# A new list order for a gated long convolution and MLP kernel, made with SyncE's issues and all transfers each in one line of measured times

## The chip, the cores and the metric

One core of one Trainium2 chip. The metric is the device time of one execution in microseconds (us), the median of the runs. PE is TensorE (PEld its weight loads), DVE is VectorE, ACT is ScalarE, POOL is GpSimd and SP is SyncE, which issues most of the DMAs.

## The reference

Everything is bf16, with S = 2048 rows of D = 512 channels. The normalized input goes through a gated long convolution (A) and is then gated by a GeGLU MLP (B) of the raw input:

```python
x  = A_q
xn = _layernorm(x)
s  = _A_ref(xn, A_k, A_v, A_shift_k, A_ssm_k, A_ssm_D)
g  = _silu(_B_ref(xn, B_w_gate, B_w_up, B_w_down))
return x + s * g

# _A_ref(q, k, v, shift_k, ssm_k, ssm_D)
kv  = (4-tap causal convolution of k along S with shift_k) * v
y_f = rfft(kv, length 2*S) * rfft(ssm_k, length 2*S)      # per channel
y   = irfft(y_f)[:S] + kv * ssm_D
return q * y

# _B_ref(x, w_gate, w_up, w_down): 512 -> 1792 -> 512
return (gelu(x @ w_gate) * (x @ w_up)) @ w_down
```

## The kernel before, in words

The 2048 rows are 16 tiles of 128 rows (t), in 4 quarters (q) of 512 rows. The kernel does two things at once and meets at the end.

*The MLP.* For each quarter, DVE takes the statistics of a tile (L811, L812), POOL the inverse root (L821, L822), and DVE writes the normalized tile XN (L825). The tile is turned to xnT: quarters 0 and 1 on PE (L844) with an eviction from PSUM, quarters 2 and 3 by a transposing DMA (L836). A unit (q, m), m = 0 to 13, is a gate stage of 4 matmuls and an up stage of 4 (through L609, a helper), a gelu on ACT into GE (L1093) and a product on DVE into HT (L1096). The down stages of a quarter follow, in three pieces per tile; ACT takes the gate's tanh (L1120) or silu (L1128), and DVE finishes it (L1122, L1130, L1131).

*The convolution* is a discrete Fourier transform of length 4096 by matmuls in two stages. The first stage multiplies with the table F1; its results go to staging in SBUF, from there to DRAM (ZH for ssm_k, ZK for kv), and come back with the axes changed (BH, BK). ssm_k is first turned on PE (Hn to HTr, L868). Groups H0 to H7 (ssm_k) use four staging slots that lie in the memory of XN and X tiles 8 to 15, so the profile shows them under these names; groups K0 to K7 (kv) use three slots (AST). The second stage works on 32x32 tiles (`tiles`, L984): stages psf0 to psf7 on ssm_k and psk0 to psk7 on kv, evicted to HS and KB. A DMA swaps the halves of HS into HW, DVE multiplies, and the inverse stages psi0 to psi7 (also L984) go through BO, ZI in DRAM and BI to the last transform psy0 to psy7, whose result DVE multiplies into G and, with the MLP's gate, into the output. The inverse table MI is made by turning TF on ACT (`m_turn`, L719) and two transposing DMAs (L995); G1 is a transposed copy of F1.

*PSUM* has 8 banks. Gate, up, down and half stages take one bank, stages of the convolution two neighbouring ones, transposes one. Evictions go through `copy` (L600 on ACT, L603 on DVE).

*What sets the order.* `S.add` collects 780 tasks, each with the engines that may run it and a planned duration. `SEQ`, a list of task numbers, gives the order in which they are emitted; a suffix b takes the second engine of a task. Each engine runs its tasks in this order, and the semaphores between engines are added by `Trk`. `Sched.run` walks the list and keeps planned times. These have one effect on the program: a task that needs a slot of a pool (PSUM banks, staging, GE, HS and others) gets the one that the plan has free first. Loads of inputs ("loads") and most other DMAs are issued by SP, the stores to ZH and ZI by ACT; `dma` (L581) is the helper of both.

In the plan of before, loads have a counter of their own, other transfers share a second one, `pipe`:

```python
elif t.nbytes:
    en = t.end
    if en < self.SHARED:
        free["loads"] += self.TAKEN
    pipe = max(pipe, en + self.DMA_LAT / 2) + t.nbytes / (self.SHARE_BW if en < self.SHARED else self.DMA_BW)
    t.end = pipe + self.DMA_LAT / 2 + (self.WAIT if en < self.SHARED else 0.0)
```

Task numbers that matter below: 130 and 131 are the copy of H6's second half and its store; 116 the copy of H4's second half; 119 and 121 the copies of H5's first quarters; 82 is `m_turn`; 226 and 221 are copies of the second halves of K1 and K0; 233 is the first stage of K3 on PE.

Of the kernel before, what the change touches and what calls it, by code (L numbers as in the profile page):

```python
# [24 lines left out]
N_WARM = 11  # L25
ORDER = "x00 h0 h1 x01 w0 w1 h2 h3 D0 w2 s0 k0 v0 x1 w3 k1 v1 d0 d1 k2 v2 k3 v3 x2 x3"
SEQ = (
# [22 lines left out]
)  # L50
NF_BANKS = 4
ISSUE = 470.0
LOAD_NS = {("x0_", 262144): 800.0, 262144: 850.0, 524288: 1350.0, ("x", 524288): 2100.0, ("h", 524288): 1400.0, ("wg", 524288): 1550.0, ("wu", 524288): 1450.0, 917504: 2620.0, ("sk", 524288): 1500.0, 344064: 1250.0, 46080: 350.0, 3072: 100.0, 1024: 200.0}
W_XT, W_SW, W_BK, W_BH, W_ZI, W_BI, W_ZK, W_MI, W_G1 = 1665000, 600000, 555000, 703000, 333000, 640000, 490000, 740000, 222000
NC_PAIRS = 4
SMALL = 1.15 * 262144
# [235 lines left out]
class Sched:  # L292
# [4 lines left out]
    LOAD_LAT = 2450.0  # L297
    HEDGE = 600.0
    DMA_BW = 370.0
    SHARE_BW = 300.0  # L300
    FIRST = {"loads": 300.0, "SP": 30500.0}
    DRAIN = 121.0
    EARLY, TAKEN, SHARED, WAIT = (2500.0, 1.6), 1400.0, 46000.0, 3300.0
    LANDS = (3850.0, 5450.0, 7050.0, 8650.0, 9600.0, 10450.0)

    def __init__(self):
        self.tasks = []
# [35 lines left out]
                t.deps.append(d)  # L343

    def run(self):
        free = dict(self.FIRST)
        pipe = 0.0
        n_loads = 0
        order = []
        pmode = 0  # L350
        for name in SEQ.split():
            t = self.tasks[int(name.rstrip("b"))]
            eng, dur = t.opts[name[-1] == "b"]
            base = 0.0
            for d in t.deps:
                base = max(base, d.end if eng == d.eng == "PE" else d.end + d.lat + (self.SEM if not d.nbytes or eng != "PE" else 400.0 if d.eng == "loads" else self.HEDGE))
            for b in t.w:
                if b.pool is not None and b.slot is None:
                    f, b.slot = b.pool.find()
                    b.pool.take(b.slot)  # L360
                    base = max(base, f + self.SEM)
            t.start, t.eng = max(base, free.get(eng, 800.0)), eng
            free[eng] = t.end = t.start + dur + (self.DRAIN if eng == "PE" and t.mode != pmode else 0.0)
            pmode = t.mode if eng == "PE" else pmode
            if eng == "loads":
                free[eng] = t.start + dur * (self.EARLY[1] if t.start < self.EARLY[0] else 1.0)
                if n_loads < len(self.LANDS):
                    free[eng] = self.LANDS[n_loads] - self.LOAD_LAT
                n_loads += 1
                t.end = free[eng] + self.LOAD_LAT  # L370
            elif t.nbytes:
                en = t.end
                if en < self.SHARED:
                    free["loads"] += self.TAKEN
                pipe = max(pipe, en + self.DMA_LAT / 2) + t.nbytes / (self.SHARE_BW if en < self.SHARED else self.DMA_BW)
                t.end = pipe + self.DMA_LAT / 2 + (self.WAIT if en < self.SHARED else 0.0)
            for b in set(t.r + t.w):
                b.left -= 1
                b.last_end = max(b.last_end, t.end + t.lat)
# [19 lines left out]
def build_kernel(nc, A_q, A_k, A_v, A_shift_k, A_ssm_k, A_ssm_D, B_w_gate, B_w_up, B_w_down, out):  # L399
    with ExitStack() as es0:  # L400
# [184 lines left out]
        def load(name, out_ap, in_ap, w_res, w_buf, nbytes, ring="SP", r=(), rb=()):  # L585
            sem = dsem("d_" + name)
            ns = LOAD_NS.get((name.rstrip("0123456789"), nbytes)) or LOAD_NS[nbytes]
            last_load[0] = S.add([("loads", ns)], lambda e: dma(ring, out_ap, in_ap, sem, r, w_res), r=rb, w=w_buf, nbytes=nbytes)
# [654 lines left out]
```

## Time and profile before

| | before |
|---|---|
| median of 3 runs | 195.75 us (195.61 to 195.95) |
| span of the profiled execution | 193.77 us |
| time around the span (median less span) | 1.98 us |
| PE busy | 189.6 us, 98% of the span |
| DVE busy | 160.6 us, 83% |
| ACT busy | 120.7 us, 62% |
| data moved by DMA | 48.14 MB, mean 248 GB/s |
| granted PE clock | 1.0 (9 of 9 tenths in all 40 slices) |

The profiled execution has no device time of its own on record; the median of the runs stands in for it beside its span. The span runs from the first to the last instruction. "Busy" is the time in which an engine executes instructions; PEld runs beside PE. The views used are the page, the table by windows, the chain of work that ended last, the groups of instructions by shape, the DMA issues and the timeline.

### The profile page before, as it was taken

What the parts mean: (1) busy time and instruction counts of PE and PEld (TensorE: products, weight loads), DVE (VectorE), ACT (ScalarE), POOL (GpSimd) and SP (SyncE); (2) the same over time, 40 slices, a digit from 0 to 9 for tenths busy, and PEclk for the clock granted to TensorE, in tenths of its full rate; (3) what the DMA queues carried; (4) which work ended last, traced back from release to release, by engine and by line L of the source; (5) the groups of instructions that cost most, each with busy time, mean ns of one, the idle gap of its engine ahead of it and who ended that gap; (6) DMA issues with size and microseconds to landing.
All of it is one profiled execution on the core that took longest, in us unless ns stands there. A gap on an engine that the chain in (4) does not pass through costs nothing.

```text
span 193.8 us, 3522 instructions
## 1 busy us (share of the span) xinstructions
PE 189.6 (98%) x1393; PEld 87.0 (45%) x1393; DVE 160.6 (83%) x246; ACT 120.7 (62%) x168; POOL 12.6 (7%) x32
## 2 busy tenths in 40 slices
PE   7999999999999999999999999999999999999993
PEld 2777444444444444443334334343344444444442
DVE  6998899899989797987996697887796871579984
ACT  5789877598794797874578666668656622150031
POOL 5322400000000000020200000000000000000000
PEclk9999999999999999999999999999999999999999
DMA  6999999999575659999999927788244305938643
GB/s 177 335 376 300 357 376 392 405 386 368 239 222 164 211 142 288 386 296 278 305 326 208 318 88 230 260 276 271 110 166 162 108 3 171 369 88 278 231 166 108
DMA packets 34502, 48.14 MB, mean 248 GB/s; under 512 B 8499, under 2 KB 27191, under 8 KB 34486
## 3 DMA queue, kind: packets, MB, share of 16 engines
q1 hardware_dynamic: 28982, 39.53, 63.1%
q10 hardware_dynamic: 5504, 8.39, 11.8%
q8 instruction: 11, 0.18, 0.4%
q14 instruction: 5, 0.04, 0.1%
HBM read 27.39 MB, written 14.68 MB: 217 GB/s over the span
## 4 chain that ended last, share of the span: by engine, by line
PE 94%; DVE 2%; DMA 2%; POOL 0%; ACT 0%; issue 0%
PE psall L609 86%; PE psall L984 5%; DMA X<-in_A_q_dram 2%; PE psall L868 1%; PE psall L844 1%; DVE XN L825 0%; DVE stats L811 0%; DVE HTr L603 0%; POOL mv L822 0%; DVE G L1131 0%; DVE G L1130 0%; ACT G L1128 0%; DVE xnT L603 0%; POOL mv L821 0%; DVE mv L812 0%
## 5 line engine op out<-in xcount | busy, mean ns | idle before, releaser
L609 PE MATMUL psall<-xnT,Wu 128*128 128x512 bf16 (+1 forms) x232 | 55.8, 372 | 0.0
L609 PE MATMUL psall<-xnT,Wg 128*128 128x512 bf16 (+1 forms) x232 | 55.5, 372 | 0.0
L609 PE MATMUL psall<-Wd,HT 128*128 128x512 bf16 (+2 forms) x238 | 52.7, 367 | 0.0
L1096 DVE TENSOR_TENSOR HT<-psall,GE 128x512 bf16<-128x512 f32 x54 | 36.2, 684 | 11.9 <-PE psall L609 10.9
L1093 ACT ACTIVATE GE<-psall 128x512 bf16<-128x512 f32 x54 | 31.2, 601 | 11.3 <-PE psall L609 9.0
L609 PEld LDWEIGHTS psall<-Wd,HT 128*128 128x128 bf16 x238 | 22.1, 98 | 26.2 <-issue 1.9
L609 PEld LDWEIGHTS psall<-xnT,Wg 128*128 128x128 bf16 x232 | 22.1, 98 | 25.8 <-issue 1.8
L609 PEld LDWEIGHTS psall<-xnT,Wu 128*128 128x128 bf16 x232 | 21.9, 98 | 25.7 <-issue 2.1
L600 ACT ACTIVATE HS<-psall 128x1024 bf16<-128x1024 f32 x15 | 14.7, 1022 | 5.2 <-PE psall L984 5.2
L600 ACT ACTIVATE BO<-psall 128x1024 bf16<-128x1024 f32 x10 | 10.0, 1023 | 10.6 <-PE psall L984 10.5
L600 ACT ACTIVATE KB<-psall 128x1024 bf16<-128x1024 f32 x10 | 10.0, 1023 | 7.7 <-PE psall L984 7.7
L965 DVE TENSOR_TENSOR KTM<-KK,SKB 128x2048 bf16<-128x2048 bf16 x12 | 14.6, 1214 | 0.1
L967 DVE TENSOR_TENSOR KAC<-KAC,KTM 128x2048 bf16<-128x2048 bf16 x12 | 14.6, 1213 | 0.0
L600 ACT ACTIVATE AST<-psall 128x1024 bf16<-128x1024 f32 x12 | 12.1, 1021 | 2.4 <-PE psall L609 2.1
L1120 ACT ACTIVATE G<-psall 128x512 bf16<-128x512 f32 x12 | 7.0, 599 | 10.4 <-PE psall L609 9.9
L1122 DVE SCALAR_TENSOR_TENSOR G<-G,psall 128x512 bf16<-128x512 bf16 x12 | 7.9, 683 | 6.3 <-ACT G L1120 6.3
L1047 DVE TENSOR_TENSOR HS<-KB,HS 128x1024 bf16<-128x1024 bf16 x16 | 10.8, 683 | 1.1 <-ACT KB L600 1.0
L603 DVE CAST BO<-psall 128x1024 bf16<-128x1024 f32 x6 | 7.3, 1225 | 5.3 <-PE psall L984 5.2
L1128 ACT ACTIVATE G<-psall 128x512 bf16<-128x512 f32 (+2 forms) x5 | 2.5, 511 | 14.1 <-PE psall L609 14.1
L811 DVE BATCH_NORM_STATS2 stats<-X 128x6 f32<-128x512 bf16 x16 | 10.4, 675 | 0.7 <-DMA X<-in_A_q_dram 0.7
L1047 DVE TENSOR_TENSOR HW<-KB,HW 128x1024 bf16<-128x1024 bf16 x16 | 10.8, 682 | 0.0
L600 ACT ACTIVATE XN<-psall 128x1024 bf16<-128x1024 f32 (+1 forms) x10 | 8.4, 856 | 2.9 <-PE psall L609 2.8
(81 smaller groups left out, 179.4 us busy)
## 6 DMA issues: line engine op xcount, KB each, us to landing
BH<-ZH SPq DMA_DIRECT2D x8, 512.0 KB, 5.8
HW<-HS SPq DMA_DIRECT2D x16, 256.0 KB, 3.0
BK<-ZK SPq DMA_DIRECT2D x8, 512.0 KB, 5.9
ZI<-BO ACTq DMA_DIRECT2D x16, 256.0 KB, 2.5
BI<-ZI SPq DMA_DIRECT2D x8, 512.0 KB, 4.5
ZK<-AST SPq DMA_DIRECT2D x6, 512.0 KB, 3.0
Hn<-in_A_ssm_k_dram SPq DMA_DIRECT2D x4, 512.0 KB, 6.4
KK<-in_A_k_dram SPq DMA_DIRECT2D x4, 512.0 KB, 10.8
```

What stands on the lines that cost most here:

```text
L600: return h.activation(o, i, ACTF.Copy, scale=scale)
L603: return h.tensor_copy(o, i)
L609: return h.matmul(o, lhsT=l, rhs=r, start=st, stop=sp)
L811: t_stats[t] = op([("DVE", 670.0)], lambda e, h, t=t: h.bn_stats(stats[:, t, :], X[:, t, :]), r=[bX[q][t % 4]], w=[bst[t]], rr=[R_X[t]], w ...
L965: op([("DVE", dur)], lambda e, h, j=j, m=m: h.tensor_tensor(KTM[:, m.slot, :, :], kk(j), sk(j), ALU.mult), r=need + [bSKB[j], a], w=[m], r ...
L967: op([("DVE", dur)], lambda e, h, m=m: h.tensor_tensor(KAC[:, a.slot, :, :], KAC[:, a.slot, :, :], KTM[:, m.slot, :, :], ALU.add), r=[m], ...
L984: trk.op("PE", lambda h: h.matmul(ps(s, i)[b, :], lhsT=wt(col)[a, :], rhs=data(col)[a, :], start=n < 16, stop=n >= len(todo) - 16, tile_po ...
L1047: return hd.tensor_tensor(o, flat(KB, kb[h]), o, ALU.mult)
L1093: op([("ACT", act(512))], lambda e, h: h.activation(GE[:, g.slot, :], bank(pg), ACTF.Gelu_apprx_tanh), r=[pg], w=[g], rr=lambda: R_bank(pg ...
L1096: op([("DVE", dve(512, 1))], lambda e, h: h.tensor_tensor(HT[:, q % 2, m, :], bank(pu), GE[:, g.slot, :], ALU.mult), r=[pu, g], w=[bHT[q][m]],
L1120: op([("ACT", act(n))], lambda e, h, g=g, pc=pc: h.activation(g, pc(), ACTF.Tanh, scale=0.5), r=[p], w=[bt], rr=lambda p=p: R_bank(p), ww= ...
L1122: op([("DVE", dve(512, 1))], lambda e, h, g=g, pc=pc: h.scalar_tensor_tensor(out=g, in0=g, scalar=1.0, in1=pc(), op0=ALU.add, op1=ALU.mult ...
```

## The change

The list `SEQ` is replaced by another order of the same 780 tasks. 22 evictions take the other of their two engines (ACT has 189 tasks instead of 185, DVE 235 instead of 239). The first eight loads keep their order. In `Sched.run`, SP's issues get one counter, and all transfers (loads, ZH and ZI stores, reads and turns) one counter `dma` in list order at 370 GB/s; the planned landings of the first six loads are replaced by 4.35 to 10.2 us, those of the profile above, and the planned time of one kind of load (the 512 KB quarters of x) goes from 2100 to 1500 ns.

The diff, with the list cut to the first of its lines:

```diff
 SEQ = (
-    "0 2 3 5 4 7 17 18 6 11 1 8 9 12 10 66 19 67 68 74 20 69 75 50 21 49 52b 13 22 76 83 87b 77 54 56b 132 51 84 133 53 70 88 71 55 125 113 111 134 "
...
+    "17 0 18 19 3 1 2 20 5 11 4 8 9 12 68 7 10 69 66 6 67 49 76 50 74 77 21 51b 84 75 53 88b 13 83 52 54 132 55 125 87 133 22 70 71 111 72 96 26 "
...
-LOAD_NS = {..., ("x", 524288): 2100.0, ...}
+LOAD_NS = {..., ("x", 524288): 1500.0, ...}
...
-    SHARE_BW = 300.0
-    FIRST = {"loads": 300.0, "SP": 30500.0}
+    AHEAD, ISSUE = 6000.0, (480.0, 3000.0)
     DRAIN = 121.0
-    EARLY, TAKEN, SHARED, WAIT = (2500.0, 1.6), 1400.0, 46000.0, 3300.0
-    LANDS = (3850.0, 5450.0, 7050.0, 8650.0, 9600.0, 10450.0)
+    LANDS = (4350.0, 5590.0, 6870.0, 8420.0, 9350.0, 10200.0)
...
     def run(self):
-        free = dict(self.FIRST)
-        pipe = 0.0
+        free = {"SP": 700.0}
+        dma = 0.0
...
-            t.start, t.eng = max(base, free.get(eng, 800.0)), eng
-            free[eng] = t.end = t.start + dur + (self.DRAIN if eng == "PE" and t.mode != pmode else 0.0)
-            pmode = t.mode if eng == "PE" else pmode
+            t.eng = eng
             if eng == "loads":
-                free[eng] = t.start + dur * (self.EARLY[1] if t.start < self.EARLY[0] else 1.0)
+                t.start = max(base, free["SP"])
+                dma = max(dma, t.start + self.LOAD_LAT) + dur
                 if n_loads < len(self.LANDS):
-                    free[eng] = self.LANDS[n_loads] - self.LOAD_LAT
+                    dma = self.LANDS[n_loads]
                 n_loads += 1
-                t.end = free[eng] + self.LOAD_LAT
-            elif t.nbytes:
-                en = t.end
-                if en < self.SHARED:
-                    free["loads"] += self.TAKEN
-                pipe = max(pipe, en + self.DMA_LAT / 2) + t.nbytes / (self.SHARE_BW if en < self.SHARED else self.DMA_BW)
-                t.end = pipe + self.DMA_LAT / 2 + (self.WAIT if en < self.SHARED else 0.0)
+                t.start = max(t.start, dma - dur - self.LOAD_LAT - self.AHEAD)
+                free["SP"] = t.start + (self.ISSUE[1] if dur > 3000.0 else self.ISSUE[0])
+                t.end = dma
+            else:
+                t.start = max(base, free.get(eng, 800.0))
+                free[eng] = t.end = t.start + dur + (self.DRAIN if eng == "PE" and t.mode != pmode else 0.0)
+                pmode = t.mode if eng == "PE" else pmode
+                if t.nbytes:
+                    t.end = dma = max(dma, t.end + self.DMA_LAT) + t.nbytes / self.DMA_BW
```

The part of the two lists that the prediction speaks of, where the store 131 follows the copy 130. Before, then after:

```
... 116 ... 130 33 27 38 131 418 414 422 140 139 416 424 ...
... 130 422 459 38 416 393 424 46 115 136 116 144 423 65 39 29 43 145 98 398 425 131 99 463 146 461 465 ... 118 ... 119 ... 121 138 ...
```

More of the change, by code (lines that the diff above doesn't have):

```diff
@@ L52 @@
 ISSUE = 470.0
-LOAD_NS = {("x0_", 262144): 800.0, 262144: 850.0, 524288: 1350.0, ("x", 524288): 2100.0, ("h", 524288): 1400.0, ("wg", 524288): 1550.0, ("wu", 524288): 1450.0, 917504: 2620.0, ("sk", 524288): 1500.0, 344064: 1250.0, 46080: 350.0, 3072: 100.0, 1024: 200.0}
+LOAD_NS = {("x0_", 262144): 800.0, 262144: 850.0, 524288: 1350.0, ("x", 524288): 1500.0, ("h", 524288): 1400.0, ("wg", 524288): 1550.0, ("wu", 524288): 1450.0, 917504: 2620.0, ("sk", 524288): 1500.0, 344064: 1250.0, 46080: 350.0, 3072: 100.0, 1024: 200.0}
 W_XT, W_SW, W_BK, W_BH, W_ZI, W_BI, W_ZK, W_MI, W_G1 = 1665000, 600000, 555000, 703000, 333000, 640000, 490000, 740000, 222000
```

42 rows, old and new, of the table SEQ are left out of this document.

## The prediction

> **What bounds the kernel now.** I read the page first (busy shares, granted clock, the chain by engine), then a table of windows, then the chain piece by piece, and last the timeline at the places where the new list differs most. The page:
>
> ```profile
> span 193.8 us, 3522 instructions
> PE 189.6 (98%) x1393; PEld 87.0 (45%) x1393; DVE 160.6 (83%) x246; ACT 120.7 (62%) x168; POOL 12.6 (7%) x32
> PEclk9999999999999999999999999999999999999999
> PE 94%; DVE 2%; DMA 2%; POOL 0%; ACT 0%; issue 0%
> ```
>
> PE is busy for 98% of the span at the full granted clock, and the chain that ended last runs through PE for 94%. Busy PE alone proves little, so the next two views ask whether any of that time is waiting. The windows (us, then busy time and count of each engine, clock, DMA share, GB/s):
>
> ```profile
> core 0: us, PE busy (x) PEld busy (x) DVE busy (x) ACT busy (x) POOL busy (x), PEclk, DMA share, GB/s
> 0.00:5.64 5.64, 4.59 (x12) 1.50 (x12) 3.81 (x16) 3.66 (x5) 3.05 (x15) 1.00 0.67 210
> 5.64:8.02 2.38, 2.24 (x19) 1.79 (x19) 2.13 (x7) 1.15 (x3) 1.39 (x3) 1.00 0.93 273
> 8.02:13.46 5.44, 5.44 (x53) 4.86 (x54) 5.21 (x12) 4.68 (x9) 1.56 (x4) 1.00 1.08 386
> 13.46:60.00 46.54, 46.54 (x243) 23.07 (x243) 44.03 (x57) 36.05 (x52) 3.70 (x6) 1.00 0.95 334
> 60.00:120.00 60.00, 60.00 (x504) 24.95 (x503) 50.03 (x79) 42.82 (x56) 2.91 (x4) 1.00 0.83 250
> 120.00:190.80 70.80, 70.79 (x569) 30.84 (x567) 54.59 (x77) 32.09 (x45) 0.00 (x0) 1.00 0.55 188
> 190.80:193.77 2.97, 0.00 (x0) 0.00 (x0) 0.84 (x4) 0.28 (x1) 0.00 (x0) 0.85 0.39 124
> ```
>
> From 8.02 to 190.80 us PE has no free time at all: 5.44 + 46.54 + 60.00 + 70.79 of 182.78 us. DVE and ACT have slack in each of these stages, tightest from 13.46 to 60 us, where DVE works 44.03 of 46.54. DMA is also tightest there, at a share of 0.95. The chain (start, us, what) says whether the matmuls keep their own pace:
>
> ```profile
> 35.70 44.47 PE psall L609 x208
> 158.28 31.75 PE psall L609 x150
> 190.05 0.50 ACT G L1128
> 190.57 0.37 DVE G L1130
> ```
>
> 208 matmuls in 44.47 us are 213.8 ns each; 150 in 31.75 us are 211.7 ns, with narrower ones among them. No wait fits between them. So the kernel is PE's work laid end to end, with a head (up to 8.02 us) and a tail (behind 190.80 us). A new order can shorten only the head and the tail. Anywhere else it can only open holes.
>
> The span is 193.77 us; the median of the runs shown is 195.75 us (195.61 to 195.95). I take the difference, 1.98 us, as lying around the span in both kernels, and the sum below starts at 195.75. About 0.2% (0.39 us) is what a measurement of this kernel can tell from no change, by the 0.34 us between its lowest and highest run.
>
> **The change part by part.** *What it is.* The planner's constants and its bookkeeping of transfers issue no instruction. What reaches the chip is the list: the order on each engine, the choice between ACT and DVE for an eviction, and the slots that follow from planned times. PE's work is the same 252 list entries, with the same 24 stages of 32x32 tiles standing apart from one another (48 changes of tile shape in either list). So PE's own sum does not move: 0.
>
> 22 evictions change engine, net 4 from DVE to ACT. These rows price one eviction of each kind (busy us, mean ns):
>
> ```profile
> L600 ACT ACTIVATE AST<-psall 128x1024 bf16<-128x1024 f32 x12 | 12.1, 1021 | 2.4 <-PE psall L609 2.1
> L603 DVE CAST BO<-psall 128x1024 bf16<-128x1024 f32 x6 | 7.3, 1225 | 5.3 <-PE psall L984 5.2
> L1093 ACT ACTIVATE GE<-psall 128x512 bf16<-128x512 f32 x54 | 31.2, 601 | 11.3 <-PE psall L609 9.0
> L600 ACT ACTIVATE xnT<-psall 128x512 bf16<-128x512 bf16 x7 | 4.2, 597 | 1.0 <-PE psall L844 0.5 <-PE psall L609 0.4
> ```
>
> Four more on ACT are at most 4 x 1.02 = 4.1 us of the 73 us in which ACT is idle, and DVE gives up 4.9 us: 0 on the path as long as their order fits, which the next points look at.
>
> *The head.* The first eight loads keep their order, so the first load of ssm_k (Hn0) still lets PE start at 5.64. In the head of before (start, us, engine, what; in brackets the idle time before it):
>
> ```profile
> 5.64 0.97 PEld L868 LDWEIGHTS psall<-ident,Hn 128*128 128x128 f32 x8 [0.70 <-DMA Hn<-in_A_ssm_k_dram]
> 6.30 0.41 DVE L825 TENSOR_SCALAR XN<-X,mv 128x512 bf16<-128x512 bf16 x1 [0.22 <-POOL mv L822]
> 6.63 0.68 DVE L603 COPY HTr<-psall 128x1024 bf16<-128x1024 bf16 x1
> 6.76 0.23 PEld L844 LDWEIGHTS psall<-ident,XN 128*128 128x128 bf16 x4 [0.16 <-DVE XN L825]
> 8.02 0.23 PEld L844 LDWEIGHTS psall<-ident,XN 128*128 128x128 bf16 x4 [0.42 <-DVE XN L825]
> ```
>
> the weight loads of the two first transposes of normalized tiles wait 0.16 and 0.42 us for DVE: 0.58 us is the most that any order can win here. In the new list tile 1 is normalized first on DVE, as before (its transpose can start at 6.77), then DVE copies HTr0_0 (0.68) and normalizes tile 0 (0.41): the second transpose can start at 6.63 + 0.68 + 0.41, about 7.7, instead of 8.02. That wins 0.3. But the first half stages of the transform of ssm_k then come up while ACT and DVE still evict. I add up the PE entries of the new list at the pace of these rows up to the first full gate stage. It would start at the same 13.46 as before with all gaps closed up to the one just named, and one half stage (H7, second half) meets a PSUM bank that ACT clears about 0.1 to 0.3 us late. I take 0, with -0.3 as the lower end (the whole win kept) and +0.1 as the upper.
>
> *The store that frees the staging.* The first stage of the transform of ssm_k is copied to one of four staging slots and stored to ZH from there, by DMAs that ACT issues. The fifth group needs the slot of the first store. In before:
>
> ```profile
> 25.33 0.34 ACTq L581 DMA_DIRECT2D ZH<-XN  x1
> ZH<-XN ACTq DMA_DIRECT2D x1, 512.0 KB, 7.2
> 32.92 1.02 ACT L600 ACTIVATE XN<-psall 128x1024 bf16<-128x1024 f32 x1 [0.59 <-PE psall L609]
> ZH<-X ACTq DMA_DIRECT2D x2, 512.0 KB, 3.1
> ```
>
> (the second row is the answer on DMAs for 25.2 to 25.6 us, the last for 50.2 to 50.6: issues, KB each, us to landing). The store (ZH6) was issued at 25.33, landed 7.2 us later at 32.5, and the fifth group's copy began at 32.92. It was that close already, and PE lost nothing by it. The new list puts two gelu entries and the second half of group H4 between the copy of H6 and its store. On PE, H4's second half stands behind H6's by one stage of 2 matmuls, two of 4 and one turned tile: 10 x 0.214 + 0.23 = 2.4 us. So ZH6 is issued at about 25.3 + 0.2 + 2.4 = 27.9 and lands, by the same 7.2, at 35.1. Behind it ACT has, before the fifth group's first copy: two copies of 1.02, five entries of 0.60 and two more stores of 0.34, 5.7 us, so it is there at 27.9 + 0.34 + 5.7, about 34, and 34.4 if it also waits for PE as the PE entries suggest. ACT then stands for some 0.7 us. Queued behind the waiting copy on ACT are its second quarter, the store ZH7, the turned tile xnT1_1 and the gelu of unit (0,9): 0.60 + 0.60 + 0.34 + 0.60 = 2.1 us to the end of the turned tile, that is 37.2. The PE stage that next wants banks, H5's second half, is due at 37.35 by the sum of PE entries, and the gate stage of unit (1,8) at 38.65. So the hole is covered by about 0.1 us if the store takes 7.2. The row 50.2:50.6, with the loads over, would make it 3.1 us and no hole at all. I take 0, the nearest row being the one of before in which ACT idled 0.59 and PE nothing; the upper end is +0.8 (a landing at 36.0).
>
> The planner now puts loads and stores on one line in list order, 512 KB at its 370 GB/s being 1.4 us each; the 7.2 against 3.1 says that a store among loads is not served in its turn. The Trainium skill ("DMA: Bandwidth & Descriptors", section "Issuing engines are not separate DMA queues") says that transfers started by different engines run on the same 16 DMA engines and interleave with each other, which speaks against planning by one line. By that rule the time would be that of rival A, 196.55, and by the planner's line the 195.95 of the sum.
>
> *The turned table.* The task m_turn (L719) turns the inverse table on ACT:
>
> ```profile
> 52.15 1.02 ACT L600 ACTIVATE AST<-psall 128x1024 bf16<-128x1024 f32 x1 [0.53 <-PE psall L609]
> 53.07 1.08 ACT L1093 ACTIVATE GE<-psall 128x512 bf16<-128x512 f32 x2
> 54.02 1.60 ACT L719 ACTIVATE TFA<-TF 128x512 bf16<-128x512 bf16 x2
> 55.49 1.56 ACT L719 ACTIVATE TFB<-TF 128x512 bf16<-128x512 bf16 x2
> 56.92 0.99 ACT L600 ACTIVATE AST<-psall 128x1024 bf16<-128x1024 f32 x1
> ```
>
> It took 54.02 to 57.05, 3.0 us, where the planner counts 2.4. Before, it stood behind the copy of K1's second half (52.15) and two gelus; in the new list it is ahead of that copy and of K0's second. K1's second half is then off PE at about 54.5 and could be copied by 55.5; behind m_turn (about 53.5 to 56.5) it is copied from 56.5 to 57.6. The PE stage K3, due at 57.4, wants the pair of banks: a hole of 57.6 - 57.4 = 0.2, from 0 (a start of m_turn 0.2 earlier) to 0.4. PE has no slack to hide it, so +0.2.
>
> *The rest.* G1's turn, bh0, the X2 and X3 loads, the transposes of xn 2 and 3, and the bk and hw transfers are moved on SP. Each is issued about as early as in before against its reader or earlier, with a microsecond or more between; inverse stage 4 goes from fifth to seventh, and stage 7 still comes last, before the last transform reads ZI: 0. What covers these is DMA's share of 0.83 and 0.55 in the two later windows. *The tail* keeps its chain, ACT 190.05, DVE 190.57, the last store: 0.
>
> Sum: 195.75 + 0 (PE) + 0 (head) + 0 (staging) + 0.2 (turned table) + 0 (rest, tail) = 195.95 us.
>
> **The rivals.** *A, slower: the staging slot.* ZH6 takes 8 us or more, lands at 35.9 or later, and ACT stands with H5's copy while PE runs out of banks at 37.35. It decides from a landing at about 35.2, one for one. For it: 7.2 us measured among loads, and the two stores ZH4 and ZH1, which the new list issues back to back at about 32.3. Against it: those two are issued when ZH6 has been under way for 4.4 us, and 7.2 was already the time among loads at a DMA share of 0.95. Price 0.6 (landing 35.8), with the turned table 0.8: 196.55 us.
>
> *B, slower: the turned table costs more.* ACT stands 3.0 us while K1's second half, K0's second half and the gelus behind wait; if two stages find no bank instead of one, the price is 0.4 + 0.2 = 0.6: 196.35 us. For it: 3.0 against the planned 2.4. Against it: only 0.2 by my sum.
>
> *C, faster: the head's win stays.* The second transpose starts 0.3 earlier and no half stage waits for a bank, while the turned table finds its bank free; with 0.1 of the first 0.16 wait also gone, 195.75 - 0.4 = 195.35 us. For it: 0.58 us of waits shown. Against it: at 13.46 my sum finds nothing left.
>
> That the change does nothing of what it says I hold for small: the list is what is emitted, and 22 evictions do change engine, so "same instructions" holds but for these.
>
> **How the numbers follow.** My forecast, no change beyond 0.2%: 0.48, its own range 195.6 to 196.14. A 0.25, B 0.17, C 0.10. Faster by over 0.2% is C, 0.10; slower A and B, 0.42; same 0.48. The range runs from 195.4 (C's edge) to 196.9 (A with a landing at 36.0, 0.8 + 0.2, and 0.15 for the spread of runs): some 6% are left out below and 10% above, where A would be larger than I price it.
>
> **What would show it.** Right: PE busy to within 0.3 us of every window from 8 us on, about 189.6 us of PE in a span near 194.0; ACT idle for 0.5 to 1 us before a copy into the staging (tile XN or X) near 34 to 35 us with a DMA as its releaser; a PE wait of some 0.2 us near 57.5 with an ACT copy as releaser. Wrong: a PE wait near 37 released by ACT (A), waits of PE above 0.4 between 54 and 60 (B), a first full gate stage before 13.3 and nothing after it (C), or any hole of over 0.3 us beyond 60 us, where I have none.

## The result and the profile after

The changed kernel is slower: 197.0 us median (196.78 the lowest of 6) against 196.0 for the kernel before in the same runs. The ratio is 1.0064 (95% interval 1.0045 to 1.0083), some 1.25 us. One execution of 200.94 us lay far above the others and is left out of the ratio. The profiled execution took 197.1 us with a span of 195.3, 1.5 us more than before. The forecast was 195.95 within 195.4 to 196.9, so the time lies 0.1 us outside its range and 1.05 above the forecast itself. The other five executions have a median of 196.89, at the range's edge, and the kernel before, 195.75 in the forecast, read 196.0 here; the difference decides more than the time alone: +0.2 us was forecast, and some 1.25 was measured. Line numbers are one less than before (L608 is the helper of L609).

The page of the changed kernel, the lines that answer to those of before:

```profile
span 195.3 us, 3520 instructions
PE 189.2 (97%) x1380; PEld 87.1 (45%) x1393; DVE 156.7 (80%) x242; ACT 123.5 (63%) x172; POOL 13.1 (7%) x32
PE 70%; DMA 16%; SPq 5%; issue 3%; DVE 3%; ACT 1%; DVEq 0%; ACTq 0%
```

PE's busy time is that of before (189.2 against 189.6; 13 matmul records are missing from this trace, all 1393 weight loads are there). What changed is the chain: PE carries 70% of it instead of 94%, and DMA 16%. The windows show where PE stood (columns as before):

```profile
8.02:13.46 5.44, 5.44 (x54) 4.68 (x52) 4.87 (x12) 5.23 (x12) 1.55 (x4) 1.00 1.08 377
13.46:30.00 16.54, 16.23 (x92) 8.51 (x90) 14.09 (x25) 12.79 (x20) 4.69 (x6) 1.00 1.06 344
30.00:40.00 10.00, 9.79 (x53) 4.97 (x55) 10.00 (x13) 7.00 (x13) 0.00 (x0) 1.00 1.05 323
40.00:50.00 10.00, 9.74 (x46) 4.24 (x45) 9.46 (x10) 7.77 (x11) 0.00 (x0) 1.00 0.96 374
50.00:60.00 10.00, 10.00 (x48) 4.56 (x47) 9.31 (x10) 8.24 (x12) 0.00 (x0) 1.00 0.56 194
80.00:100.00 20.00, 19.14 (x201) 7.77 (x203) 16.19 (x36) 15.19 (x19) 2.56 (x4) 1.00 1.04 298
100.00:120.00 20.00, 20.00 (x194) 8.17 (x193) 14.33 (x22) 14.86 (x22) 0.00 (x0) 1.00 0.98 286
```

In this profile the head up to 13.46 us is as full as before, 50 to 60 us as well; 13 to 50 and 80 to 100 us have holes. In the timeline of PE these rows stand at them, each with the row ahead (start, us, engine, what; in brackets the idle time before, which is less than the time lost, because an end of a matmul is drawn with its pipeline):

```profile
26.16 1.03 PE L608 MATMUL psall<-HTr,F 128*128 128x512 bf16 x4
27.40 1.04 PE L608 MATMUL psall<-xnT,Wu 128*128 128x512 bf16 x4 [0.21 <-DMA Wu<-in_B_w_up_dram]
...
29.57 0.39 PE L843 MATMUL psall<-ident,XN 128*128 128x128 bf16 x4
30.16 1.04 PE L608 MATMUL psall<-xnT,Wu 128*128 128x512 bf16 x4 [0.20 <-DVE HT L1095]
...
44.00 0.59 PE L608 MATMUL psall<-HTr,F 128*128 128x512 bf16 x2
44.80 0.60 PE L608 MATMUL psall<-HTr,F 128*128 128x512 bf16 x2 [0.21 <-ACT X L599]
...
88.74 1.89 PE L608 MATMUL psall<-Wd,HT 128*128 128x512 bf16 x8 [0.16 <-issue]
91.02 0.44 PE L983 MATMUL psall<-BK,TF 32*32 32x512 bf16 x16 [0.39 <-DMA BK<-ZK]
```

From start to start, at 0.216 us for a matmul of 512 columns and 0.22 for a turned tile, the lost time is 27.40 - (26.16 + 4 x 0.216) = 0.38, 30.16 - (29.57 + 0.22) = 0.37 and 44.80 - (44.00 + 0.43) = 0.37. The fourth is 0.46: the nine down matmuls ahead took 2.05 in the kernel before, and here the first of them starts at 88.51. Together 1.58 us, against 1.5 in the span. The reasons named are: the load u3, which lands at 27.35; a bank that DVE frees at 30.1; a copy on ACT that waited for a store to ZH; and bk0, which lands at 90.89.

The copy on ACT, and one before it:

```profile
36.41 1.29 ACT L599 ACTIVATE XN<-psall 128x512 bf16<-128x512 f32 x2 [1.19 <-PE psall L843]
43.72 1.02 ACT L599 ACTIVATE X<-psall 128x1024 bf16<-128x1024 f32 x1 [0.77 <-DMA ZH<-X]
```

The first is H5's first quarter. The releaser named, a turned tile on PE, had long ended; the store ZH6 was issued at 26.80 and landed at 36.33, 0.08 us before the copy began. So this is the staging slot, put down to another engine. The second is H2's copy behind ZH1, issued at 32.70 and landed at 43.64.

Why were the stores late? The answer on DMAs for 25 to 28.5 us gives ZH6 9.5 us to land, 7.2 before:

```profile
ZH<-XN ACTq DMA_DIRECT2D x1, 512.0 KB, 9.5
```

And in the answer for the whole span, the transpose of F1 to G1 (64 KB, task 175), which the new list issues among the loads, took 11.9 us, where the kernel before had 4.6:

```profile
G<-F SPq DMA_TRANSPOSE x1, 11.9
```

The windows around its landing (35.2 us), of the changed kernel:

```profile
30.00:32.00 2.00, 1.84 (x12) 1.02 (x13) 2.00 (x3) 1.82 (x3) 0.00 (x0) 1.00 1.40 333
32.00:34.00 2.00, 2.00 (x12) 0.93 (x10) 2.00 (x3) 0.60 (x1) 0.00 (x0) 1.00 0.66 114
34.00:36.00 2.00, 2.00 (x13) 1.03 (x11) 2.00 (x4) 1.08 (x2) 0.00 (x0) 1.00 1.08 349
```

From 32 to 34 us the DMA engines are busy for 0.66 and move 114 GB/s, with loads and stores queued; the windows beside it move 333 and 349. Over 30 to 35 us it is 243 GB/s against 392 before; the 149 GB/s that are missing make 0.75 MB in 5 us, 1.9 us of transfer at 392. The last load (V1) lands at 49.65 instead of 47.85.

### The profile page after: what moved, and what is told of

Read it like the earlier page. It is cut to its first block, busy times and chain, and to the rows that moved or that the text cites. A ratio compares the mean times of both kernels' runs of the same rounds, so it can differ in the third digit from the quotient of the medians.

```text
span 195.3 us, 3520 instructions
## 1 busy us (share of the span) xinstructions
PE 189.2 (97%) x1380; PEld 87.1 (45%) x1393; DVE 156.7 (80%) x242; ACT 123.5 (63%) x172; POOL 13.1 (7%) x32
## 3 DMA queue, kind: packets, MB, share of 16 engines
q10 hardware_dynamic: 5504, 8.39, 11.9%
## 4 chain that ended last, share of the span: by engine, by line
PE 70%; DMA 16%; SPq 5%; issue 3%; DVE 3%; ACT 1%; DVEq 0%; ACTq 0%
PE psall L608 65%; DMA KK<-in_A_k_dram 6%; DMA ZH<-X 6%; SPq L580 5%; PE psall L983 5%; DMA BK<-ZK 3%; DMA ZK<-AST 1%; DVE KAC L960 1%; DVE KAC L966 1%; DVE HT L1095 1%; ACT AST L599 1%; ACT X L599 1%; DVE G L1130 0%; DVE G L1129 0%; ACT G L1127 0%
## 5 line engine op out<-in xcount | busy, mean ns | idle before, releaser
L608 PE MATMUL psall<-xnT,Wg 128*128 128x512 bf16 (+1 forms) x232 | 55.7, 372 | 0.0
L608 PE MATMUL psall<-xnT,Wu 128*128 128x512 bf16 (+1 forms) x232 | 55.0, 372 | 0.4 <-DMA Wu<-in_B_w_up_dram 0.2
L608 PE MATMUL psall<-Wd,HT 128*128 128x512 bf16 (+2 forms) x229 | 51.6, 366 | 0.8 <-issue 0.6
L608 PEld LDWEIGHTS psall<-Wd,HT 128*128 128x128 bf16 x238 | 22.0, 98 | 26.3 <-issue 2.1
L608 PEld LDWEIGHTS psall<-xnT,Wu 128*128 128x128 bf16 x232 | 22.2, 98 | 26.0 <-DMA Wu<-in_B_w_up_dram 0.7
L608 PEld LDWEIGHTS psall<-xnT,Wg 128*128 128x128 bf16 x232 | 21.6, 98 | 25.9 <-issue 2.8
L599 ACT ACTIVATE HS<-psall 128x1024 bf16<-128x1024 f32 x16 | 15.6, 1022 | 3.9 <-PE psall L983 3.8
L599 ACT ACTIVATE KB<-psall 128x1024 bf16<-128x1024 f32 x12 | 12.0, 1022 | 7.2 <-PE psall L983 7.2
L1046 DVE TENSOR_TENSOR HW<-KB,HW 128x1024 bf16<-128x1024 bf16 x16 | 10.9, 683 | 0.0
L599 ACT ACTIVATE X<-psall 128x1024 bf16<-128x1024 f32 (+1 forms) x9 | 8.4, 937 | 2.4 <-PE psall L608 1.6
```

What stands on the lines that cost most here:

```text
L599: return h.activation(o, i, ACTF.Copy, scale=scale)
L608: return h.matmul(o, lhsT=l, rhs=r, start=st, stop=sp)
L1046: return hd.tensor_tensor(o, flat(KB, kb[h]), o, ALU.mult)
```

## The experiments

Theories. **Deadline:** each hole puts PE at a time fixed by something that PE does not drive (a landing, a DVE chain); removing one leaves the next to set the same lag. **Additive:** each hole costs its own length. Beside these: G1 is behind all of it, the plan's slots, or the order of stores on ACT. The kernels of a set ran on the same chip beside the kernel before; sets are compared with care, as chips differ. Where "slots held" is said, a table gives every buffer the slot that it has in the changed kernel. Losses of PE are worked out as above, from starts.

**First set: one part undone at a time.** Only list entries move; slots are those of the changed kernel. The changed kernel itself did not run beside this set, nor beside the second and the fourth. Its ratio to the kernel before is 1.0064, 1.0054 and 1.0097 on three other occasions, so in these sets a gain under some 0.3% could not be told from none.

G1 back behind the load of X2:

```diff
- ... 465 175 151 ... 176 ...
+ ... 465 151 ... 175 176 ...
```

> The changed kernel with one entry of its list moved: the transpose of F1 to G1 (task 175) goes back behind the load of X2, where the kernel before had it; all slots stay the same. Deadline theory (each hole of PE sets PE's lag to one fixed landing, and the last one decides): the stores ZH4 and ZH1 land about 2 us earlier (7 to 8 us from issue instead of 9.2 and 10.9), the wait of 0.8 us of ACT for a landed store near 43.7 us goes, and with it PE's hole of 0.37 us at 44.8 us; the holes at 27.4 us (late u3), 30.2 us (DVE) and 90.9 us (bk0) stay. Time 0.3 to 0.4 us below the changed kernel, 196.6. Theory that G1 is behind all of it: u3 lands about 0.7 us earlier too, and the time falls by 0.7 or more, to 196.3 or less. Theory that the order of the stores on ACT makes them late, not G1: ZH1 still lands later than 43 us, time 197.0.

Measured: ratio to before 1.0049 (1.0023 to 1.0076), profiled span 194.3. ZH6 takes 6.6 us, ZH1 lands at 42.0 and V1 at 47.74. The four holes of the first profile are not in this one. First the windows from 30 us:

```profile
30.00:32.00 2.00, 2.00 (x17) 1.03 (x15) 2.00 (x2) 2.00 (x4) 0.00 (x0) 1.00 1.06 391
32.00:34.00 2.00, 2.00 (x12) 1.03 (x11) 2.00 (x4) 0.64 (x2) 0.00 (x0) 1.00 1.03 385
34.00:36.00 2.00, 2.00 (x14) 1.03 (x13) 2.00 (x3) 1.57 (x3) 0.00 (x0) 1.00 1.08 395
```

385 GB/s from 32 to 34 us instead of 114, so the gap in the transfers is G1's. The order of the stores is not what lengthens ZH6: it is the same here. ZH1 is another matter. It still takes 9.4 us here (9.0 to 10.2 in the seven kernels with the new list and G1 late, 10.9 in the changed kernel), while the first four stores of the kernel before took 6.0 to 7.5, so two stores issued back to back may be a part of its time; no run parts them. u3 lands at 27.41, as late as before the move, so G1 is not behind that one. I had expected the holes at 27.4, 30.2 and 90.9 us to stay. That the first two are gone is not G1's doing: PE came to u3 later, having waited 0.40 us for the first gate weights:

```profile
9.84 1.03 PE L608 MATMUL psall<-xnT,Wg 128*128 128x256 bf16 x8 [0.24 <-DMA Wg<-in_B_w_gate_dram]
```

The stage with u3 starts at 27.63 instead of 27.40. The median does not show the gain of the profile: the 12 executions run from 195.76 to 198.48.

u3 ahead of g2:

```diff
- ... 28 414 130 422 459 38 ...
+ ... 38 28 414 130 422 459 ...
```

> The changed kernel with the load u3 moved ahead of the load g2 and nothing else; all slots stay the same. Both theories: u3 lands near 25.9 us instead of 27.35, and PE's wait of 0.7 us (0.38 us of lost time) for it at 27.4 us goes. Additive theory (each hole costs its own length): the time falls by 0.38 us, to 196.6. Deadline theory: the next hole is set by DVE, which frees the bank at 30.1 us whatever PE does before, so that hole grows from 0.37 to 0.75 us and the time stays at 197.0 within 0.1.

Measured: 1.0077 (1.0051 to 1.0103). u3 lands at 25.23 and its wait is gone. DVE's bank still comes at 29.5 and costs 0.2, H5's second half 0.2, and bk0 0.62. No gain can be seen, as the deadline theory says; its size for the second hole (0.75) was wrong, since in this execution k's second load landed 0.7 earlier and DVE's chain with it.

The product of unit (0,5) ahead of the first KAC:

```diff
- ... 143 59 129 28 414 130 422 459 38 416 393 ...
+ ... 393 143 59 129 28 414 130 422 459 38 416 ...
```

> The changed kernel with the product of unit (0,5) (task 393) moved ahead of the first shift product KAC (task 143) on DVE, so that DVE does it in the 1.64 us in which it waits for the taps and for the second load of k; slots held as in the changed kernel. Both theories: the product of unit (0,13), which frees the bank, ends 0.6 us earlier, near 29.4 us, and PE's wait of 0.37 us at 30.15 us goes. Additive theory: the time falls by 0.37 us, to 196.6. Deadline theory: the store ZH1, which lands at 43.6 us, sets the same lag as before, its hole grows to 0.75 us, and the time stays at 197.0 within 0.1.

Measured: 1.0078 (1.0047 to 1.0109). The expectation fell in part: the product of unit (0,13) ends at 29.75, not 29.4, and the hole shrinks to 0.26 only. The first KAC still starts at 24.65, in the changed kernel at 24.64. There it followed the second load of k, which landed at 24.46. Here this load landed at 24.14, but the moved product stood in the way: DVE waited 0.98 us for PE's stage of unit (0,5) and ended the product just ahead of KAC.

```profile
24.04 0.69 DVE L1100 TENSOR_TENSOR HT<-psall,GE 128x512 bf16<-128x512 f32 x1 [0.98 <-PE psall L613]
24.65 1.63 DVE L965 TENSOR_TENSOR KAC<-KK,SKB 128x2048 bf16<-128x2048 bf16 x1
```

What DVE does behind it is one chain of 1.2 us products. No gain in time can be seen.

A down piece ahead of psk0:

```diff
- ... 522 259 523 ... 261 535 ...
+ ... 522 535 259 523 ... 261 ...
```

> The changed kernel with one down piece of 5 matmuls (task 535, 1.08 us) moved on PE ahead of the stage psk0, which waits 0.48 us for the read bk0; all slots stay the same. Both theories: psk0 then starts near 91.5 us with bk0 landed at 90.9, the wait goes, and since no later hole is bound by a fixed landing, the time falls by 0.4 to 0.5 us, to 196.5. Theory that the plan's slots or the three earlier holes alone set the end: no change, 197.0, with the wait moved to a stage behind it.

Measured: 1.0097 (1.0064 to 1.0130), no gain that can be seen. The wait at psk0 went and came back behind it (0.17 us at psk2, 0.45 at the down piece that follows). At H5's second half (40.2 us) PE lost 1.14 us behind the staging. This profile also holds something that no profile above has:

```profile
21.23 1.02 PE L867 MATMUL psall<-ident,Hn 128*128 128x128 f32 x7 [1.18 <-DMA Hn<-in_A_ssm_k_dram]
```

PE waits 1.2 us for the load Hn2, landing at 21.09. In the changed kernel's profile it landed at 19.22 for a use at 19.33; before, at 16.43 for a use at 17.25.

**Second set: plan or list, and G1 alone.**

The old list under the new plan (the diff with the list left as it was):

> The changed kernel's plan (one line for SP's issues, one for all transfers, the new landings) under the old list; 193 of the PSUM slots differ from the kernel before. Theory that the order is all: same as the kernel before, 195.9, PE without a hole. Theory that the slots from the new plan matter: a PE wait on an eviction of another bank somewhere, 0.2 to 0.5 us slower.

Measured: 1.0009 (0.9995 to 1.0024): no difference. Its profile (span 194.6) has one hole, 0.8 us at 20.6 for u1, which landed at 20.56 in that execution and at 19.08 in the profile of before.

The new list under the old plan (only the list of the diff):

> The old plan under the new list; 117 PSUM slots differ from the changed kernel. Theory that the order is all: as the changed kernel, 0.5 to 0.8% above the kernel before, with waits of PE near 27.4 (u3), 30 (DVE), 37 or 44 (staging behind a store) and 90.5 us (bk0). Theory that slots matter: one of these waits gone, or another one.

Measured: 1.0061 (1.0036 to 1.0086), like the changed kernel, with holes at H5's second half (37.9 us, 0.19) and psk0 (90.5 us, 0.38) and ZH6 at 9.2 us. The holes at u3 and at DVE's bank, which I expected near 27.4 and 30 us, are not in its profile. So the order is the cause; the plan's slots are worth 0.24% at most, by the interval of the run before.

The kernel before, with G1 alone moved among the loads:

```diff
- S.add([("SP", ...)], g1, ..., after=last_load)
+ S.add([("SP", ...)], g1, ..., after=() if ww is R_G1 else last_load)
- ... 35 41 42 ... 47 175 176 ...
+ ... 35 175 41 42 ... 47 176 ...
```

> The kernel before with the transpose of F1 to G1 alone moved up among the loads, ahead of the load of Wd0 (issued near 22 us); all slots stay the same, and the list's entry no longer has to follow the last load. Theory that G1 costs the transfers beside it about 2 us: what lands behind it lands 1.5 to 2 us later, ZH6 near 34.3 instead of 32.5 us, ACT stands about 1.4 us before the copy of H2 at 32.9 us, PE loses 0.3 to 1 us there, time 196.2 to 196.9. Theory that the stores are late by the new order on ACT: ZH6 lands within 0.5 us of 32.5 and the time is that of the kernel before.

Measured: 1.0015 (0.9997 to 1.0033). By its interval the time is not clearly apart from the kernel before, but the mechanism is all there. ZH6 takes 9.9 us and lands at 35.11. The copy of H2 and then PE stand. First the answer on DMAs, then 30 to 35 us of the windows:

```profile
ZH<-XN ACTq DMA_DIRECT2D x1, 512.0 KB, 9.9
```

```profile
30.00:35.00 5.00, 5.00 (x24) 2.25 (x23) 5.00 (x6) 2.25 (x4) 0.00 (x0) 1.00 0.81 233
```

The timelines of ACT and of the weight loads:

```profile
35.19 1.02 ACT L600 ACTIVATE XN<-psall 128x1024 bf16<-128x1024 f32 x1 [2.95 <-PE psall L609]
...
36.27 0.55 PEld L609 LDWEIGHTS psall<-xnT,Wg 128*128 128x128 bf16 x4 [0.83 <-ACT XN L600]
```

ACT idles 2.95 us, again put down to PE, and begins 0.08 us behind the landing. PE waits 0.83 for it.

Four moves together: G1 late, u3 first, the product of unit (0,5) first, 535 ahead of psk0:

> The changed kernel with four entries moved and the slots held: G1 behind the load of X2, u3 ahead of g2, the product of unit (0,5) ahead of the first KAC, the down piece 535 ahead of psk0. Deadline theory: no hole of over 0.1 us is left, the time is that of the kernel before within 0.1%, 195.8 to 196.0, not below it, since PE's own work bounds both. Additive theory: 1.5 us less than the changed kernel, 195.5. Theory that another cause is open: a hole stays or a new one opens, 196.3 or more.

Measured: 1.0050 (1.0032 to 1.0067). The times of both theories failed; 196.3 or more was to mean that another cause is open, and so it is. The two moves that failed alone say where: DVE's bank still costs 0.61 at 30 us, and behind psk0 the moved down piece opens holes of 0.62 us in all.

**Third set: a better move for DVE.** The changed kernel again, G1 late again, G1 late with u3 first, and these two with the product of unit (0,13) ahead of the second KAC sum:

```diff
- ... 145 98 398 425 ...
+ ... 425 145 98 398 ...
```

> The changed kernel itself once more, beside the next three on the same chip, because single executions so far spread by 1 to 2 us. Deadline theory: 0.5 to 0.8% above the kernel before; the four waits of PE (u3 near 27, DVE near 30, a staging slot near 37 or 44, bk0 near 90.5 us) come back, each with another size.

> G1 behind the load of X2, as in the first experiment, nothing else. Theory that G1 among the loads is the largest part: 0.3 to 0.5 us below the changed kernel on this chip, no wait of PE for the staging near 37 and 44 us and for bk0. Theory that it is one of four equal holes: 0.1 us or less below it, as the late u3 and DVE still set the lag.

> G1 behind the load of X2 and the load u3 ahead of g2, slots unchanged. Deadline theory: u3's wait goes, the wait on DVE at 30 us grows to 0.6 us, and the time is that of G1 alone within 0.1 us. Additive theory: another 0.38 us less.

> G1 behind the load of X2, u3 ahead of g2, and on DVE the product of unit (0,13) ahead of the second KAC sum (task 425 ahead of 145), so that it frees its bank near 29.1 us instead of 30.1; slots held as in the changed kernel. Deadline theory: with all three holes up to 50 us gone, only bk0 is left, and the time is 0 to 0.3 us above the kernel before, 0.8 to 1.2 us below the changed kernel. Theory that something else is open: 0.5 us or more above the kernel before.

| kernel | median us | ratio to before | holes in its profile, us |
|---|---|---|---|
| changed | 197.36 | 1.0054 (1.0030 to 1.0078) | g0 0.46, DVE's bank 0.39, psk0 0.79, two stages behind it 0.61 |
| G1 late | 196.90 | 1.0033 (0.9997 to 1.0069) | g0 0.82, psk0 0.52, two stages behind it 1.04 |
| G1 late, u3 first | 197.20 | 1.0044 (1.0016 to 1.0072) | DVE's bank 0.19, psk0 1.25 |
| these and (0,13) earlier | 196.31 | 1.0008 (0.9978 to 1.0038) | g0 0.46, psk0 0.25 |

The kernel before had 196.29 here; g0 are the first gate weights. Of the four holes that I had expected in the changed kernel, two came back, DVE's bank and psk0. psk0 waits with G1 late as well, so that wait is not G1's. With the three causes moved away (G1, u3, DVE's bank), the loss is gone within the interval, which is wide: single executions of the kernel before ran from 195.43 to 197.89 on this chip. u3 on top of G1 brings nothing that can be measured, as the deadline theory has it. Whether G1 alone is worth 0.2% stays open: the intervals overlap.

**Fourth set: bk0.**

K6's second half and psf0 each one stage earlier on PE:

```diff
- ... 508 250 ... 480 251 179 ...
+ ... 250 508 ... 179 480 251 ...
```

> The changed kernel with two stages moved up on PE by one stage of 4 matmuls (0.86 us) each: the second half of K6 ahead of the up stage of unit (1,10), and psf0 ahead of the up stage of unit (1,3); slots held. Theory of the place on PE: ZK6 lands 0.8 us earlier, bk0 too, and the wait before psk0 falls from 0.5 to 0.8 us to 0 to 0.1; the time falls by 0.4 to 0.8 us against the changed kernel, to about 0.2% above the kernel before. Theory of the shared transfers: bk0 still lands as late as before, since bh2 and hw0 move up with it; the wait stays.

Measured: 1.0103 (1.0065 to 1.0141). In the profiled execution Hn2 landed at 21.41 and PE lost 1.4 us there and 1.75 behind the staging, so its sum says nothing on bk0. bk0 took 5.1 us and cost nothing, but a gate stage at 87.3 us waited 0.34, put down to DVE, a new hole.

hw0 behind bk2 on SP:

```diff
- ... 272 182 273 ... 262 284 ...
+ ... 272 284 182 273 ... 262 ...
```

> The changed kernel with the swap hw0 behind the read bk2 on SP instead of ahead of it; all slots stay the same. Theory of the shared transfers: bk0 takes 5.5 us or less from its issue and the wait before psk0 falls to 0.1 or less, though the product with hw0 may then come late. Theory of the place on PE: bk0 keeps its 6.2 us or more, as it was issued ahead of hw0, and the wait stays.

Measured: 1.0100 (1.0074 to 1.0125). bk0 takes 5.9 us instead of 6.7, and psk0 no longer waits; waits of 0.95 us at 98.3 to 99.3 and of 0.73 at 106.0 stand there instead, both put down to DVE, which I did not take apart. This profile also lost 0.55 us at g0 and 0.54 at H5's second half. So hw0 beside bk0 may be a part of bk0's length, and moving it brings nothing.

The three moves of the third set with those of e9:

> The four moves together: G1 behind the load of X2, u3 ahead of g2, the product of unit (0,13) ahead of the second KAC sum, and the two stages of e9 moved up; slots held as in the changed kernel. Deadline theory: no wait of over 0.15 us left; the time is that of the kernel before within 0.15%, and not below it by more than that. If a wait is left, the theory lacks a cause.

Measured: 1.0032 (1.0011 to 1.0053), profiled span 194.2. psk0's wait is gone (bk0 4.2 us), and a gate stage at 83.3 us waits 0.34 instead. The expected 0.15% was missed: bk0's wait was traded for another.

**Fifth set: the load Hn2.** The changed kernel a third time, Hn2 ahead of the first load of k, and this with the three moves of the third set:

```diff
- ... 24 ... 31 ... 25 ...
+ ... 24 ... 25 31 ...
```

> The changed kernel once more beside the next two: 0.5 to 0.8% above the kernel before, by both theories, with some executions at 198 or more.

> The changed kernel with the load Hn2 one place earlier, ahead of the first load of k; all slots unchanged. Theory that the landings' lack of slack makes the spread: Hn2 lands near 18 us, 1.3 us before its use, the executions at 198 us and more get rare, and the median falls by 0.2 to 0.5 us, though the four holes stay in a profile. Theory that Hn2's late landing was only one disturbed execution: median and spread as the changed kernel within 0.15 us.

> G1 behind the load of X2, u3 ahead of g2, the product of unit (0,13) ahead of the second KAC sum, Hn2 ahead of the first load of k; slots held as in the changed kernel. Both theories: only bk0's wait of 0.1 to 0.5 us is left, 0 to 0.2% above the kernel before. By the theory of slack the spread is that of the kernel before (1 to 2 us), by the other it stays as wide as the changed kernel's.

Measured: changed 197.66, 1.0097 (1.0067 to 1.0127); Hn2 earlier 197.24, 1.0079 (1.0055 to 1.0103); with the three moves 196.12, 1.0019 (1.0001 to 1.0037), against 195.9 before. Hn2 now lands at 18.3 us, 1.1 us ahead of its use, but the executions still reach 198.31: its landing was not what makes most of the spread. The two last kernels differ by the three moves, and their intervals lie clear of each other: G1 late, u3 first and (0,13) earlier are together worth some 0.6% here. That is the firmest proof in time that the loss is in these moves of the list. Not all waits are gone with them: the profile of this kernel has 0.31 us at 22.5 for another load of gate weights and 0.30 at bk0, where I expected bk0's alone. No kernel of the 18 runs is faster than the kernel before.

The profile of the changed kernel in this set has the hole where rival A had put it, at H5's second half:

```profile
39.42 0.11 PEld L608 LDWEIGHTS psall<-HTr,F 128*128 128x128 bf16 x2 [1.09 <-ACT XN L599]
```

Here PE lost 0.77 us behind ZH6, which landed at 38.00, and 1.13 at g0, which landed at 10.22.

Over all profiles, ZH6's time to land (us) sorts by one thing:

| G1 | kernels | ZH6 to land | V1 landed |
|---|---|---|---|
| among the loads, new list | 10 | 9.2 to 10.7 | 49.3 to 51.7 |
| among the loads, old list | 1 | 9.9 | 50.9 |
| late, new list | 7 | 6.5 to 7.2 | 47.4 to 48.7 |
| late, old list | 2 | 6.6, 7.2 | 47.9, 48.5 |

From 30 to 36 us the DMA engines move 121 to 266 GB/s in the eleven kernels with G1 among the loads and 390 to 396 in the nine with G1 late. At 392 that is 1.9 to 4.1 us of transfers, and the first profile of the changed kernel has the mildest case. DMA's busy share doesn't show it: it is 1.04 to 1.06 in ten of the eleven. In the ten with the new list ACT stands 1.2 to 3.2 us for the staging slot before H5's first copy, and in seven of them PE then loses 0.2 to 1.7 us at H5's second half. In the seven with the new list and G1 late, neither happens.

One place I had overlooked: the load g0. In 8 of the 17 profiles with the new list PE loses 0.26 to 1.13 us at 9.5 to 10.4 us for it, in none of the three with the old list. It lands at 9.14 to 10.22 in those 17, at 9.33 to 9.38 in these three. The first eight loads stand in the same order in both lists, but PE can come to this stage sooner in the new one, so a part of these waits is time won before it. Net of that, the first full gate stage starts at 13.23 to 14.26 us with the new list and at 13.30 to 13.46 with the old. Whether the list is the cause of g0's late landings stays open.

And the slack from landing to use, before and after, in the two first profiles (us). At u3, ZH6 and bk0 the engine after it stood waiting; at u1 and Hn2 the use came just behind the landing in this profile and PE lost nothing:

| landing | before | after |
|---|---|---|
| u1 | 1.5 | 0.11 |
| Hn2 | 0.8 | 0.11 |
| u3 | 2.4 | 0.05 |
| ZH6 | 0.4 | 0.08 |
| bk0 | 0.9 | 0.10 |

## Why the prediction was right or wrong

**What bounds the kernel** was right: PE's own sum did not move, a new order could only open holes, and in the first profile the loss is four of them.

**The head** (0, from -0.3 to +0.1) was right in the two first profiles: 5.44 of 5.44 us busy from 8.02 to 13.46 in both. In part that was luck: in the two later profiles of the changed kernel PE waits 0.46 and 1.13 us there, at g0, which the forecast does not mention, and the first full gate stage starts at 13.38 and 14.26 instead of the forecast 13.46. **The tail** was right: ACT's last large silu at 191.58 and DVE's product at 192.10 keep the distance of 0.52.

**The turned table** (+0.2) was wrong, and rival B with it. `m_turn` did take 3.0 us (54.01 to 57.04), and K1's copy stood behind it, but that copy ended at 57.90 with K3 due at 58.20. In the kernel of five moves, with PE 1 us less late, it is 56.73 and 57.03: 0.3 us of cover where I had a hole of 0.2. I had let `m_turn` start at 53.5; it started at 52.84 there.

**The staging slot** (0, up to +0.8) had the right mechanism and the wrong size: 7.2 us was the store's time in the kernel before, and it was 9.5. A second error made up for half of this: the store was issued at 26.80, not at 27.9, and so landed at 36.33 instead of 35.1. ACT stood 1.19 us where I had 0.7, and PE lost 0.37 at the next slots in one profile and 0.2 to 1.7 at the stage I had named in seven of the ten with the new list and G1 among the loads. Rival A's price (0.6) is near. Its reason (two stores issued back to back) does not hold for ZH6: with G1 away, the same two stores follow it, and it takes 6.5 to 7.2 us.

**The rest** (0) is the step that failed. It passed G1 over in one clause, as "issued about as early or earlier": earlier was the harm, as it shares the engines with the loads. It rested on DMA's share of 0.83 and 0.55 in the two later windows, but the new list issues G1 at 23.34 us, in the window whose share it had read as 0.95. It gave a microsecond of slack to the moved transfers and did not go through the loads at all: u3, u1 and Hn2 lost theirs. It looked at transfers against their readers, and not at DVE, whose chain of KAC products starts when the second load of k lands and holds a bank behind it. And bk0's slack of 0.9 us was spent: psk0 stands 0.87 us earlier in PE's list (by the sum of entries), while bk0 took 6.65 instead of 5.6 us. The 0.46 us lost there are the sign of being wrong that the prediction had named for itself, a hole of over 0.3 us beyond 60 us.

The rule of interleaving that the prediction quoted from the Trainium skill ("DMA: Bandwidth & Descriptors") fits: at the plan's 370 GB/s the store is 1.4 us, and among loads it took 6.5 to 10.7. Another sentence of the skill falls short here: "Advanced Engine Details and Errata", section "X-Bar Transpose (TRN2)", says that transposing DMAs are as fast as regular ones; here, with one of 64 KB among loads, 1.9 to 4.1 us of the transfers beside it were lost. No run put a regular transfer of 64 KB in its place.

What stays open: the share of each hole in the median, since single executions spread more than a hole is long; why g0 is late in 8 of the 17 profiles with the new list; and bk0's time, 5.9 and 6.7 us in two executions of the kernel with G1 late and 7.4 with u3 first besides, of which hw0 may be a part.

## What to carry to other kernels

Where the matmul engine has no free time, a new order is judged by the slack of every landing against its use, loads of inputs first; a plan that leaves 0.1 us turns each us of a late transfer into lost time. Holes that are set by landings don't add up: removing one shows the next, so remove them in the order of time, and look for the one thing that makes several late. A releaser named for a wait is only the last semaphore that the profile can see: compare the start with the landings of DMAs.

## What the runs showed of the hardware

A transposing DMA of 64 KB, issued among queued loads, held the DMA engines to 114 GB/s over 2 us (385 in the same window without it), to 121 to 266 over 30 to 36 us in eleven profiles (390 to 396 in the nine without it there), and lengthened a 512 KB store beside it from 6.5 to 7.2 us to 9.2 to 10.7. Landings of the same load in the same list moved by up to 3.0 us from one execution, or chip, to another (Hn2 from 18.4 to 21.4 us in kernels of the new list that do not move it; 18.8, 19.2 and 20.7 in three executions of the changed kernel), which is more than any hole studied here.
